# Attention scores as quarter matmuls, gate logits summed once per route group, and moved gate and route products

## The chip, the core and the metric

One core of one Trainium2 chip runs the whole program. The metric is device time in microseconds (us) of one execution. The core has five engines with instruction streams of their own: TensorE (PE, whose weight loads the profile shows as PEld), VectorE (DVE), ScalarE (ACT), GpSimd (POOL) and SyncE (SP, which here only issues transfers). Each runs its own instructions in the order in which they stand, and waits for the others by semaphores. 16 DMA engines move the data.

## The reference

Attention over mean-pooled keys and values, then a mixture of experts with one expert per token. Inputs are f32; tokens are B * S = 4608, in 36 tiles of 128.

```python
batch, n_heads, seq, head_dim = (8, 8, 576, 64)
N, D, E, F = (4608, 512, 8, 1024)

k_p = k.reshape(B, H, Sp, pool, D).mean(axis=3)      # Sp = 72 pooled positions
v_p = v.reshape(B, H, Sp, pool, D).mean(axis=3)
scores = scale * np.matmul(q, k_p.transpose(0, 1, 3, 2))
attn = np.exp(scores - np.max(scores, axis=-1, keepdims=True))
attn = attn / (np.sum(attn, axis=-1, keepdims=True) + 1e-09)
x = np.matmul(attn, v_p)                             # to [4608, 512]

do_compute = (x @ w_skip) > 0
logits = x[do_compute] @ w_gate
e_idx = np.argmax(logits, axis=1)
gate_w = softmax(logits)[chosen]
out = x;  out[do_compute] += gate_w * (relu(xc @ w1[e]) @ w2[e])   # e = e_idx per token
```

## The kernel before

**Attention** runs tile by tile, t = 0 to 35, one loop iteration per tile (line 842). Work of three tiles overlaps in an iteration. PE computes the scores of tile t (L303), the values of tile t - 2 (L341, L344) and the transposes of the probabilities of tile t - 1 (L323, L324). DVE divides tile t - 3 by its sums and takes the row minima (L309) of tile t. ACT copies the transposed probabilities out of PSUM (`turned_p`, L328) and computes the eight exponentials of tile t (L315). Keys stand block-diagonally (`kbd`), two heads per matmul: K = 128 rows of which each head uses 64, 144 columns. A batch is 4.5 tiles, so tiles 4, 13, 22 and 31 hold half of one batch and half of the next; there scores and values are computed for 64 tokens at a time (`parts`), with 64 of the array's columns. An f32 matmul is one instruction in the program and two passes in the profile.

**Per batch** the keys are summed over the pool by DVE (`sum_k`, L208) and the values by POOL (`sums`, L248, then `values_both`, L271), from loads that SP issues seven to eight tiles before the batch's first tile. The value sums are transposed by PE (`turn_v`), copied by ACT (`turned_v`, L267) and multiplied with the gate weights (`gates_pe`, L278; `gates_dve`, L281 and L284), so that the values matmul also gives, per head, the nine gate logits of a token.

**Routing** goes by groups of tiles, `GROUPS = [9, 5, 4, 6, 5, 4, 3]`. `normalised` scales the logits of each tile (L359), writes x to the output and sums the logits over heads into `lg` (L362). When a group's last tile is done, `route` is queued: DVE finds each token's expert, PE counts tokens by matmuls (L397 to L401, the *products*), DVE makes the table positions (`r_di`, L406) and the payment (L408), and POOL writes one table row per token with an indirect DMA per tile (L415), 36 in all. The steps are generators, and `routes.step`, `routes.exponentials` and `routes.products` advance them at fixed places of the iteration.

**What sets the order.** Nothing is reordered on the chip; a small planner in the program decides in which iteration optional work stands. `act`, `dve` and `gps` hold items with a first tile, a last tile and an assumed cost, and each iteration takes items up to a budget (ACT 1.0, DVE 1.5, later 1.0, POOL 3.2). `Spaced.take` for POOL puts table writes between other items, with clears of the ring (L768) as filling late on. All loads are on SP's queue, by `loads[t]` at the start of iteration t.

**After the loop** the last tiles are finished, PE starts on 384 near tokens (`tile_steps`: x against the first expert, three f32r matmuls per step), and `slots` computes from the counts which table rows are needed. POOL gathers them (L1040) when all table writes have landed; PE transposes them (L1072), at a fixed place, behind 84 of the near tokens' matmuls; DVE makes the slot numbers. With these the experts' loop starts, which gathers tokens, multiplies (L1383 to L1409) and scatters results until the end.

## Time and profile before

| | |
|---|---|
| time, median of 3 runs (lowest to highest) | 480.29 us (479.85 to 484.28) |
| the profiled execution: time, span of its instructions | 481.24 us, 479.2 us |
| PE busy, share of the span | 463.5 us, 97% |
| PEld, DVE, ACT, POOL busy | 417.1, 303.4, 225.7, 250.3 us |
| mean granted clock of TensorE | 0.999 of 2.4 GHz |
| DMA moved | 103.88 MB, mean 217 GB/s |

Attention fills the first 147 us; the near tokens and the routing's end reach to about 185 us; the rest is the experts' loop. A row of the timeline gives start, duration, engine, line, operation and tiles, shapes and the number of merged instructions; in brackets stands how long the engine was idle before and for whom it waited. PE's durations include the time until a result is out, so matmuls that follow each other overlap in them; the step from one start to the next is what PE spends on one. Sums of busy time are averages over stages with different limits.

### The profile page before, as it was taken

Reading aid. Unit: us, or ns where it says so; the run is one execution under the profiler, and the core shown is the slowest. Engines: PE = TensorE matmul, PEld = TensorE weight load, DVE = VectorE, ACT = ScalarE, POOL = GpSimd, SP = SyncE. Lnnn points to the kernel's source line nnn. Section 1 sums busy time; section 2 is a strip of 40 time slices with the busy share of each in tenths; the row PEclk is TensorE's granted clock in tenths of the full one; section 3 lists DMA queues with packets and bytes.
Section 4 is the critical chain, followed back from the end, with each engine's and each line's share of the span. In section 5 each row is a group of like instructions: output and inputs, shape, how many; then the busy total and the mean of one; then the engine's idle time right before and its main releaser. Section 6 shows DMA issues by size and latency. Waiting matters only on the chain. (4 is left out here: it accounts for less than half of the span.)

```text
span 479.2 us, 11182 instructions
## 1 busy us (share of the span) xinstructions
PE 463.5 (97%) x3043; PEld 417.1 (87%) x3044; DVE 303.4 (63%) x713; ACT 225.7 (47%) x578; POOL 250.3 (52%) x328
## 2 busy tenths in 40 slices
PE   7999999999999999899999999999999999999995
PEld 4799899989999979798989987989899898989894
DVE  5877888798788622578795667663846554343321
ACT  5678768888891211546462645612435251212110
POOL 4499499999998154363342424362624161515242
PEclk9999999999999999999999999999999999999999
DMA  8999999996931026679787497877687223322021
GB/s 278 388 396 390 361 352 332 384 333 207 328 122 68 11 62 215 230 228 308 247 289 244 136 290 241 300 240 251 202 256 262 89 95 101 129 66 88 22 88 42
DMA packets 52042, 103.88 MB, mean 217 GB/s; under 512 B 10031, under 2 KB 22959, under 8 KB 50336
## 3 DMA queue, kind: packets, MB, share of 16 engines
q1 hardware_dynamic: 40544, 78.18, 47.8%
q0 software_dynamic: 11456, 25.22, 15.0%
q8 instruction: 17, 0.28, 0.2%
q14 instruction: 25, 0.20, 0.1%
HBM read 80.85 MB, written 31.21 MB: 234 GB/s over the span
## 5 line engine op out<-in xcount | busy, mean ns | idle before, releaser
L1289 POOL DMA_INDIRECT out<-ring,slot x33 | 35.8, 1085 | 109.3 <-POOLq L1115 105.6
L315 ACT ACTIVATE e<-sc,mn 128x72 f32<-128x72 f32 x288 | 65.0, 345 | 7.4 <-DVE mn L309 6.8
L1527 ACT ACTIVATE hhi<-psl 128x256 fp32r<-128x256 f32 (+3 forms) x59 | 23.5, 400 | 94.0 <-ACTq L1115 93.5
L1384 PE MATMUL psl<-xlo,w1hi 128*128 128x256 f32 (+3 forms) x220 | 64.1, 291 | 0.0
L1383 PE MATMUL psl<-xhi,w1hi 128*128 128x256 f32 (+3 forms) x220 | 64.0, 291 | 0.0
L1385 PE MATMUL psl<-xhi,w1lo 128*128 128x256 f32 (+3 forms) x220 | 64.0, 291 | 0.0
L1284 POOL DMA_INDIRECT ring<-out,slot x42 | 46.6, 1109 | 22.6 <-issue 22.4
L341 PE MATMUL o<-vbd,pT 128*128 128x148 f32 (+1 forms) x312 | 49.4, 298 | 1.1 <-DVE x L360 1.1
L1626 DVE SCALAR_TENSOR_TENSOR hlo<-psl,hhi 128x256 fp32r<-128x256 f32 (+2 forms) x55 | 23.2, 423 | 41.3 <-DVEq L1115 39.0
L415 POOL DMA_INDIRECT table<-pay,r_di x36 | 36.7, 1018 | 12.6 <-DVE mb L443 6.4
L1383 PEld LDWEIGHTS psl<-xhi,w1hi 128*128 128x128 f32 x220 | 41.3, 188 | 0.8 <-issue 0.4
L1384 PEld LDWEIGHTS psl<-xlo,w1hi 128*128 128x128 f32 x220 | 41.3, 188 | 0.5
L341 PEld LDWEIGHTS o<-vbd,pT 128*128 128x128 f32 (+1 forms) x312 | 38.6, 179 | 3.6 <-ACT ring L213 1.0
L1385 PEld LDWEIGHTS psl<-xhi,w1lo 128*128 128x128 f32 x220 | 41.2, 187 | 0.0
L1297 POOL DMA_DIRECT2D sorted<-ring x39 | 22.2, 572 | 32.9 <-DMA ring<-out,slot 25.8
L1603 DVE TENSOR_TENSOR w2lo<-stage,w2hi 128x1024 fp32r<-128x1024 f32 x28 | 34.3, 1223 | 6.6 <-DVEq L1115 6.4
L1384 PE MATMUL psd<-xlo,w1hi 128*128 128x256 f32 (+3 forms) x132 | 38.4, 291 | 0.0
L1385 PE MATMUL psd<-xhi,w1lo 128*128 128x256 f32 (+3 forms) x132 | 38.4, 291 | 0.0
L1383 PE MATMUL psd<-xhi,w1hi 128*128 128x256 f32 (+3 forms) x132 | 38.4, 291 | 0.0
L1409 PE MATMUL mb<-w2hi,hlo 128*128 128x512 f32 x88 | 34.8, 396 | 0.0
L1409 PE MATMUL psf<-w2hi,hlo 128*128 128x512 f32 x88 | 34.8, 396 | 0.0
L1407 PE MATMUL psf<-w2hi,hhi 128*128 128x512 f32 x88 | 34.8, 395 | 0.0
(276 smaller groups left out, 1216.0 us busy)
## 6 DMA issues: line engine op xcount, KB each, us to landing
stage<-in_w SPq DMA_DIRECT2D x64, 512.0 KB, 5.5
sorted<-ring POOLq DMA_DIRECT2D x39, 256.0 KB, 3.3
out<-x SPq DMA_DIRECT2D x36, 256.0 KB, 5.4
stage<-in_k SPq DMA_DIRECT2D x6, 1152.0 KB, 8.8
blocks<-sorted SPq DMA_DIRECT2D x100, 64.0 KB
qt<-in_q SPq DMA_DIRECT2D x9, 512.0 KB, 7.4
hhi<-in_vm SPq DMA_DIRECT2D x4, 1024.0 KB, 7.7
hlo<-in_vm SPq DMA_DIRECT2D x3, 1024.0 KB, 9.8
```

The source lines that it names most:

```text
L315: nc.scalar.activation(ev[:, h // 2, k0:k0 + SP], sc[:, h * SP:(h + 1) * SP], AF.Exp, bias=mn[:, 4 * i + h:4 * i + h + 1], scale=-1.0)
L341: nc.tensor.matmul(o_[sl, g * 2 * VA:(g + 1) * 2 * VA], pT[:, 2 * a + g, sl], vbd[b % 2][:, 2 * a + g, :], start=(g == 0), stop=False)
L415: m = nc.gpsimd.indirect_dma_start(table, bass.IndirectOffsetOnAxis(ap=di[:, j:j + 1], axis=0), flat(fin["pays"][:, t0 + j:t0 + j + TW // ...
L1284: g.indirect_dma_start(ring[:, (s + 3) % 9, 0:D], None, out, bass.IndirectOffsetOnAxis(ap=slot[:, s:s + 1], axis=0), bounds_check=NTOK - 1 ...
L1289: g.indirect_dma_start(out, bass.IndirectOffsetOnAxis(ap=offsets, axis=0), ring[:, (s + 3) % 9, 0:D], None, bounds_check=NTOK - 1, oob_is_ ...
L1383: t.matmul(ps, whi[0][:, k, w], xhi[:, k, xs], start=(k == 0), stop=False)
L1384: t.matmul(ps, whi[0][:, k, w], xlo[:, k, xs], start=False, stop=False)
L1385: last = t.matmul(ps, wlo[0][:, k, w], xhi[:, k, xs], start=False, stop=(k == 3))
L1407: t.matmul(ps, hhi[:, k, sl], whi[1][:, k, :], start=(k == 0), stop=False)
L1409: last = t.matmul(ps, hlo[:, k, sl], whi[1][:, k, :], start=False, stop=(k == 7))
L1527: a.activation(hhi[:, f, xs], bank(f, xs, alone), AF.Relu).then_inc(sem["act"], 1)
L1603: v.tensor_tensor(chunk_of(wlo, c), chunk_view(stage[c], c), chunk_of(whi, c).bitcast(F32), ALU.subtract).then_inc(sem["wlo1" if c < 4 els ...
```

## The change

Scores of tiles 3 to 33 are computed in quarters. `scores` now issues 16 matmuls per tile in place of 4: for each of four head pairs, two halves of the tokens by two heads, each with 64 rows (one head's dimensions), 64 tokens and 72 columns. The two row halves write two PSUM tiles. The first three and last two tiles keep the old form (`by_halves`). `exped` follows the new places of the heads.

The transposed probabilities are copied in two pieces, of 384 and 256 columns (`turned_p`), into two tiles; the order of the transposes is changed so that the first three fill the first piece. The gate product's PSUM place moves from `mb` to `pt`, and one temporary of the routing from PSUM to SBUF.

`normalised` keeps the scaled logits of a whole group in one tile and sums them over heads once, with the group's last tile.

In the iteration, `routes.exponentials` comes first; `gates_pe` stands behind the values; `gates_dve` moves into the next iteration; the route's products stay before the exponentials only if they were already due at the start of the iteration, and otherwise stand behind the values. The load of the first weight chunk stands behind the tile's output, ACT takes up to two items in the iteration before a batch starts, and assertions state that a chunk's place is free in program order. `slots` cuts its small tiles out of a query buffer.

```diff
+        group = sp.tile([128, GMAX, H, 9], F32, name="l8")
...
+        def by_halves(t):
+            return t < 3 or t > NT - TILES
...
+        def scores(t):
+            if by_halves(t):
+                return [scores_by_halves(t, i) for i in range(2)]
+            sc = [ps_s.tile([128, 512], F32, name="sc")[:, 0:4 * SP] for _ in range(2)]
+            for g in range(4):
+                for i, sl in enumerate(halves):
+                    b = (t * 128 + i * 64) // S
+                    for r, o in zip(halves, range(2)):
+                        nc.tensor.matmul(sc[o][sl, g * SP:(g + 1) * SP], qts[t // QG][r, t % QG, g, sl],
+                                         kbd[b % 2][r, g, o * SP:(o + 1) * SP], start=True, stop=True)
+            return sc
...
         def turn_p(e):
             for i in range(2):
                 k0 = (4 * SP + GAP + 2 * KL) * i
                 ev = e[:, k0:k0 + 256].rearrange("p (k g) -> p g k", g=2)
                 for g in range(2):
-                    nc.tensor.transpose(ptf[:, (2 * i + g) * 128:(2 * i + g) * 128 + 128], ev[:, g], ident)
-            nc.tensor.transpose(ptf[:, 512:640], e[:, 256:384], ident)
+                    nc.tensor.transpose(pt[:, i, (2 * i + g) * 128:(2 * i + g) * 128 + 128], ev[:, g], ident)
+                if i == 0:
+                    nc.tensor.transpose(pt[:, 0, 256:384], e[:, 256:384], ident)

         def turned_p():
-            pT = ap.tile([128, 5, 128], F32, name="pT")
-            nc.scalar.activation(flat(pT), ptf[:, 0:640], AF.Copy)
+            pT = [ap.tile([128, 3 - i, 128], F32, name=f"pT{i}") for i in range(2)]
+            for i, sl in enumerate((slice(0, 384), slice(256, 512))):
+                nc.scalar.activation(flat(pT[i]), pt[:, i, sl], AF.Copy)
             return pT
...
-            nc.vector.tensor_reduce(lg[:, t, :], l8.rearrange("p h c -> p c h"), axis=AX.X, op=ALU.add)
+            if t + 1 in ends:
+                nc.vector.tensor_reduce(lg[:, t0:t + 1], group[:, 0:n8].rearrange("p j h c -> p j c h"), axis=AX.X, op=ALU.add)
...
-            at(wload(cc), lambda cc=cc: load_first(cc))
+            (loads if cc else behind).setdefault(wload(cc), []).append(lambda cc=cc: load_first(cc))
...
             new = turns.get(t)
+            known = routes.held
+            routes.exponentials()
             if t > 3:
                 pts[t - 2] = turned_p()
...
-            routes.exponentials()
             if t > 2:
                 normal(t - 3)
-                sc = [scores(t, i) for i in range(2)]
+                if t - 1 in turns:
+                    gates_dve(turns[t - 1])
+                for f in behind.pop(t, ()):
+                    f()
+                sc = scores(t)
...
-            if new is not None:
-                gates_pe(new)
...
+            elif known:
+                routes.products()
             else:
-                routes.products()
-            spent = act.take(t, 0.4 if new is not None else 0.0, 1)
+                routes.exponentials()
+            spent = act.take(t, 0.4 if new is not None else 0.0, 2 if t + 1 in FIRST[2:] else 1)
             exponentials(t, sc, mn)
             os_[t - 2] = values(t - 2, pts.pop(t - 2))
+            if new is not None:
+                gates_pe(new)
+            fresh = t < NT - 1 and routes.products()
             if 2 < t < NT - 1:
                 turn_p(es.pop(t - 1))
...
             while t < NT - 1 and busy < (DVE if t < PICKED else DVEL) and routes.step():
-                busy += 0.24
+                busy += 9 if fresh else 0.24
```

Two places show what moves. The first is PE's stream at tile 5, where batch 1's gate product is made. `pt` holds transposed probabilities, `sc` scores, `o` values; `vs` and `ls` are value sums, `wgs` the gate weights. Before:

```order
L323 MATMUL pt<-cfs,e_127 128x128 x4
L324 MATMUL pt<-cfs,e_127 128x128
L261 MATMUL pt<-cfs,vs 128x128 x2
L262 MATMUL pt<-cfs,ls_133 128x128
L303 MATMUL sc<-ring,xhi 128x144 x4
L278 MATMUL mb<-wgs,vT 128x36 x3
L341 MATMUL o<-vbd_120,pT 128x148 x2
L344 MATMUL o<-ring,pT 128x2x74
L341 MATMUL o<-vbd_120,pT 128x148 x2
L344 MATMUL o<-ring,pT 128x2x74
```

The same place of the change:

```order
L340 MATMUL pt<-cfs,e_128 128x128 x2
L342 MATMUL pt<-cfs,e_128 128x128
L340 MATMUL pt<-cfs,e_128 128x128 x2
L262 MATMUL pt<-cfs,vs 128x128 x2
L263 MATMUL pt<-cfs,ls_134 128x128
L318 MATMUL sc<-ring,xhi 64x72 x16
L360 MATMUL o<-vbd_120,pT_442 128x148 x2
L363 MATMUL o<-ring,pT_442 128x2x74
L360 MATMUL o<-vbd_120,pT_443 128x148 x2
L363 MATMUL o<-ring,pT_442 128x2x74
L279 MATMUL pt<-wgs,vT 128x36 x3
```

The scores are 16 quarters instead of 4 matmuls, the third transpose is the fifth of before, and the gate product has gone from between scores and values to behind the values.

The second place is POOL's stream around the first table write. `hlo` holds batch 4's loaded values here, `vl` the rest of them; `vbd_121` is the end of batch 3's work. Before:

```order
L271 TENSOR_TENSOR vbd_121<-vs,cfs 128x8x64
L415 DMA table<-pay,r_di 36864x8
L248 TENSOR_TENSOR hlo<-hlo 128x512
L415 DMA table<-pay,r_di 36864x8
L248 TENSOR_TENSOR hlo<-hlo 128x512
L415 DMA table<-pay,r_di 36864x8
```

The same place of the change:

```order
L272 TENSOR_TENSOR vbd_121<-vs,cfs 128x8x64
L249 TENSOR_TENSOR hlo<-hlo 128x512 x2
L249 TENSOR_TENSOR vl_129<-vl_129 96x256
L436 DMA table<-pay,r_di 36864x8
L249 TENSOR_TENSOR hlo<-hlo 128x512
L436 DMA table<-pay,r_di 36864x8
```

Three sums of batch 4 that stood between and behind the first writes now stand ahead of the first one. From there to the gather both streams hold the same number of each kind of instruction.

## Rows read from the trace of the kernel before

**Rows 1.** Windows by stretch: length, busy time of each engine (instructions), clock, DMA, GB/s

```profile
20.00:57.00 37.00, 35.99 (x305) 33.73 (x305) 29.79 (x91) 28.12 (x102) 27.98 (x39) 1.00 1.02 395
180.00:479.00 299.00, 291.71 (x1749) 261.50 (x1748) 166.94 (x263) 108.62 (x183) 115.85 (x151) 1.00 0.56 187
```

**Rows 2.** Around L1072: PE's timeline, the last write, the gather, and their landing times

```profile
146.97 0.43 PE L532 MATMUL sc<-xhi,w1hi 128*128 128x384 f32 x1
155.03 0.98 POOL L415 DMA_INDIRECT table<-pay,r_di  x1 [0.30 <-issue]
table<-pay,r_di POOLq DMA_INDIRECT x1, 2.1
158.10 1.08 POOL L1040 DMA_INDIRECT stage<-table,s_coli  x1 [2.08 <-DVE s_last L1060]
DMA to landing us min/median/max: 4.0/4.0/4.0
162.82 0.34 PE L1072 MATMUL o<-cfs,stage 81*128 81x81 f32 x2
```

**Rows 3.** POOL's stretch of table writes: the window, and its first write

```profile
55.78:156.05 100.27, 98.01 (x820) 92.55 (x819) 83.38 (x302) 75.25 (x251) 92.21 (x108) 1.00 0.76 266
55.78 1.08 POOL L415 DMA_INDIRECT table<-pay,r_di  x1 [6.39 <-DVE mb L443]
```

**Rows 4.** Batch 4's values: issue on SP, landing, first sum on POOL; DMA behind it

```profile
46.89 0.38 SPq L221 DMA_DIRECT2D hlo<-in_vm  x1
hlo<-in_vm SPq DMA_DIRECT2D x1, 1024.0 KB, 9.8
56.90 1.29 POOL L248 TENSOR_TENSOR hlo<-hlo 128x512 f32<-128x512 f32 x1
56.00:58.00 2.00, 2.00 (x25) 1.70 (x24) 1.90 (x9) 1.08 (x3) 1.97 (x2) 1.00 0.68 256
```

**Rows 5.** Timeline of PE and ACT over one undisturbed tile

```profile
67.63 0.27 PE L324 MATMUL pt<-cfs,e 128*128 128x128 f32 x1
67.74 1.15 PE L303 MATMUL sc<-ring,qt 128*128 128x144 f32 x8
68.00 0.70 ACT L328 ACTIVATE pT<-pt 128x640 f32<-128x640 f32 x1 [0.59 <-PE pt L324]
68.76 0.77 PE L341 MATMUL o<-vbd,pT 128*128 128x148 f32 x4
70.37 0.63 PE L323 MATMUL pt<-cfs,e 128*128 128x128 f32 x4
70.84 0.27 PE L324 MATMUL pt<-cfs,e 128*128 128x128 f32 x1
```

**Rows 6.** PE's timeline in half-batch tiles: scores by half widths, values, and back

```profile
56.73 0.27 PE L262 MATMUL pt<-cfs,ls 128*128 128x128 f32 x1
56.94 1.20 PE L303 MATMUL sc<-ring,xhi 128*64 128x144 f32 x16
66.83 0.29 PE L344 MATMUL o<-ring,pT 128*64 128x148 f32 x1
67.05 0.74 PE L323 MATMUL pt<-cfs,e 128*128 128x128 f32 x4
```

**Rows 7.** A wait (us, times, longest), and the small sums by form

```profile
PEld mb L278 <- ACT vT L267: 1.4, 4, 0.4
L362 DVE TENSOR_REDUCE lg<-l 128x9 f32<-128x72 f32 x32 | 8.7, 273 | 0.0
```

**Rows 8.** PE at the start and the end, and the clock of the last stretch

```profile
1.73 5.47 PE L739 MATMUL o<-ring 128*128 128x512 f32 x6 [1.73 <-POOL ring L717]
10.94 1.02 PE L817 MATMUL o<-ring 128*128 128x512 f32 x2
473.89 0.40 PE L1409 MATMUL psf<-w2hi,hlo 128*128 128x512 f32 x1
478.00:479.20 1.20, 0.00 (x0) 0.00 (x0) 0.00 (x0) 0.00 (x0) 0.00 (x0) 0.54 0.34 128
```

More of the change, by code (lines that the diff above doesn't have):

```diff
@@ L348, in normalised @@
             x = ap.tile([128, H, HD], F32, name="x", bufs=5)
-            l8 = ap.tile([128, H, 9], F32, name="l8")
+            t0, n8 = next(ends[e] for e in sorted(ends) if e > t)
+            l8 = group[:, t - t0]
             rc = ap.tile([128, 2, 4], F32, name="rc")
@@ L408, in route @@
                     lambda: nc.vector.reciprocal(pay[:, t0:t0 + n, 1], se)]
-            for a, b in zip(ranked, paid) if last else zip(paid, ranked):
+            for a, b in zip(ranked, paid) if last else (paid, ranked):
                 a()
@@ L670, in take @@
                         break
-        loads, turns = {}, {}
+        loads, behind, turns = {}, {}, {}
+        lows = []
         act, dve, gps = Work(ACT), Work(DVE), Spaced(GPS)
@@ L812, in exponentials @@
             es[t] = ebuf[t % 2]
-            for i in range(2):
-                exped(es[t], sc[i], mn, i)
+            for n in range(2):
+                exped(es[t], sc[n], mn, n, by_halves(t))
         def constant_product():
@@ L836, in attention @@
         gates_dve(0)
-        sc = [scores(2, i) for i in range(2)]
+        sc = scores(2)
         mn = softmax(2, sc)
@@ L852, in attention @@
                 turned_v(new, tp)
-            routes.exponentials()
             if t > 2:
                 normal(t - 3)
-                sc = [scores(t, i) for i in range(2)]
+                if t - 1 in turns:
+                    gates_dve(turns[t - 1])
+                for f in behind.pop(t, ()):
+                    f()
+                sc = scores(t)
             if t == NT - 1:
@@ L954, in attention @@
         spare = lambda: ps_o.tile([128, 2, 512], F32, name="o")[:, 0].rearrange("p (i n) -> p i n", i=4)
-        for wait in slots(tc, nc, c, offs, table, near, bufs, out, fin, ap, spare):
+        for wait in slots(tc, nc, c, offs, table, near, bufs, out, fin, flat(qp.tile([128, QG, 4, 128], F32, name="qt").rearrange("p a g n -> p (a g) n")), spare):
             if wait:
@@ L977, in slots, with new @@
     rows, slot, gate, nti = (fin[n] for n in ("rows", "slot", "gate", "nti"))
-    new = lambda name, dt=F32: p.tile([128, NE], dt, name="s_" + name)
-    n = new("n"); ni = new("ni", I32); half = new("half", I32); odd = new("odd", I32); units = new("units")
-    three = new("three", I32); wide = new("wide", I32); end = new("end"); zero = new("zero"); le = new("le")
-    le1 = new("le1"); w = new("w"); more = new("more")
-    none = new("none"); kind = new("kind"); own = new("own")
-    cf = p.tile([128, 1], F32, name="s_cf")
-    cd = p.tile([128, 1], F32, name="s_cd")
-    ends = p.tile([128, UNITS, NE], F32, name="s_ends", bufs=1)
-    last = p.tile([128, UNITS, NE], F32, name="s_last", bufs=1)
-    short = new("short")
-    row = p.tile([128, UNITS], F32, name="s_row", bufs=1)
-    edge = p.tile([128, UNITS], F32, name="s_edge", bufs=1)
-    col = p.tile([128, 4], F32, name="s_col")
-    coli = p.tile([128, 1], I32, name="s_coli")
+    at = [0]
+    def new(w=NE, dt=F32):
+        at[0] += -(-w // 8) * 8
+        got = p[:, at[0] - -(-w // 8) * 8:][:, 0:w]
+        return got if dt == F32 else got.bitcast(dt)
+    n, units, end, zero, le, le1, w, more, none, kind, own, short = (new() for _ in range(12))
+    ni, half, odd, three, wide = (new(dt=I32) for _ in range(5))
+    cf, cd, col, coli = new(1), new(1), new(4), new(1, I32)
+    row, edge = new(UNITS), new(UNITS)
+    ends, last = (new(UNITS * NE).rearrange("p (u e) -> p u e", e=NE) for _ in range(2))
     nc.vector.memset(zero, 0.0)
```

40 lines of the change are left out of this document (22 added, 18 removed).

## The prediction

> **What bounds the kernel now.** I read the windows by stretch first. PE is busy in 35.99 of 37 us in the early tiles and in 291.71 of 299 us in the experts behind 180 us [rows 1], so whatever moves the start of the experts moves the end, one for one. The question is what sets that start. PE comes out of attention at 146.97 us [rows 2] and fills the time with 84 matmuls of the near tokens. Then, in its own order, stands the transpose of L1072, which reads the rows that POOL's gather of L1040 fetches from the table. POOL may issue that gather only when the last of 36 table writes has landed. So two paths meet at L1072: PE's (attention, then 84 matmuls) and POOL's (table writes, gather). The reader should compare their arrivals: the last write starts at 155.03 and lands 2.1 later, the gather starts at 158.10 and lands 4.0 later, at 162.1; PE reads at 162.82 [rows 2]. The paths are level to within 0.7 us.
>
> How full is POOL's path? From the first table write to the end of the last it is a stretch of 100.27 us (55.78 to 156.05) with POOL busy in 92.21 [rows 3]; the 8.1 left are spread over 108 instructions, and I saw no wait above 0.31 there. Before it POOL stood idle for 6.39 us, waiting for the first route [rows 3]. The second instruction of the stretch, the first sum over batch 4's values (hlo, 56.90), is near its own limit too: its load was issued at 46.89 and landed 9.8 later, at 56.7 [rows 4]. The 16 DMA engines are full (share 1.02 over 20 to 57 us [rows 1]) and fall to 0.68 only behind 56 [rows 4].
>
> **The change on PE.** An undisturbed tile takes 67.63 to 70.84 = 3.21 us from last transpose to last transpose [rows 5]: 0.11 to the scores, 1.02 until the values, 1.61 for the values, 0.47 for four transposes. The scores are 8 passes (an f32 matmul is two) in 1.15 with a tail of 0.29 (the duration of the single half-width matmul of [rows 6] stands for it), so 0.86 / 7 = 0.123 a pass of 144 columns. Quarters make them 32 passes of 72 columns, 0.061 each by scaling, and if the four quarters run at once, 8 steps. No row shows four; the half-batch tiles show two: 16 half-width passes took 1.20 against 1.15 for 8 full ones, 0.05 more [rows 6]. That gives 7 x 0.061 + 0.05 = 0.48. Changing the array's shape costs: 0.21 from the last full transpose to the first half-width matmul instead of 0.11, and 0.22 from the last half-width matmul (148 columns) to the next full one [rows 6]; with 72 columns I take 0.16. New tile: 0.21 + 0.48 + 0.16 + 1.61 + 0.47 = 2.93, 0.28 less. The copy of the probabilities (0.70, ended at 68.70, 0.06 before the values started) was the values' gate [rows 5]; it is split in two, and the first part can start after three of five transposes, so it ends before 2.93 needs it. 31 tiles change (3 to 33). 27 of them save 0.28 = 7.6. Four half-batch tiles already paid for the shape: 0.21 + 0.91 becomes 0.21 + 0.48, 0.43 each = 1.7. The gate products move behind the values, and the route's products too unless they were already due: that takes away waits like the 1.4 for the values' copy [rows 7], which with its smaller neighbours comes to 3.8; I take 3, bounded by 0 and 3.8. Sum on PE: 12.3. Copies, buffers and POOL's sums, for which the transposes of the values wait, will take some of it back: 5 to 12, and I take 6.5.
>
> **The change on DVE and ACT.** 32 of the 36 small sums over heads took 0.273 each [rows 7]; seven larger ones replace them, at most the same 9.8 us in all. DVE is busy in 29.79 of 37 us [rows 1], so the gain lies beside PE's work and I cost it at nothing. If that cover goes, DVE is earlier, not later. ACT's copies move the same 640 columns; even if each half took the whole copy's 0.70 [rows 5], ACT has 37 - 28.12 = 8.9 us free there [rows 1] over some ten tiles, 0.89 each. I cost it at nothing too.
>
> **The change on POOL.** The number of sums, clears and writes from there to the gather is the same. But three sums over batch 4 (two of 512 columns and one of 256) now stand ahead of the first write. Before, POOL could write while that load was on its way. Now it waits for the load, and all of the 100.27 us lies behind it. If the load lands at 56.7 as before, POOL ends at 56.9 + 100.27 = 157.2 instead of 156.05: +1.1. How much earlier can it land? It is issued at the start of tile 11, which PE reaches at most 3.0 earlier (7 x 0.28, one half-batch tile 0.43, two gate waits of 0.3). So the bounds are 53.9 and 56.9. The load has the bytes of all earlier loads ahead of it, and with the engines full an earlier issue only lengthens the queue; so I take 56.6, by the row with share 1.02 [rows 1]. The Trainium skill (DMA: Bandwidth & Descriptors, Queues, rings and completion order) says that the descriptors of one ring are consumed in order; by it alone the load would land at 56.7, and POOL's shift would be +1.1 instead of +0.8. This case's trace agrees as far as the share goes. POOL's shift: +0.8 (bounds -1.9 and +1.1). PE's slack at L1072 is between 0 and 0.7; I take 0.4. Rows are read 0.4 later than now.
>
> **What late rows do to PE.** PE reaches its transpose at 162.8 - 6.5 = 156.3 and waits there until 163.2: some 7 us with no matmul (5.4 to 12.4 by the gain's bounds). The clock does fall after a pause: the last matmul starts at 473.89, and the mean granted clock of 478 to 479.2 is 0.54 of 2.4 GHz [rows 8], which is mostly the lower level, 1.2 GHz. At the start of the kernel six passes of 512 columns took 5.47, where later two took 1.02 [rows 8], so a pass stood at about 0.85 against 0.43, and the start lost 2.7 us. Price of a fall here: 0 to 2.7. I take 2.2, near the start's row, since these matmuls follow each other without a break and should end the slow stretch a bit sooner.
>
> **Sum.** +0.4 +2.2 = +2.6. The profiled execution took 481.24, of which the span is 479.2 and 2.0 lies around it; it stands 0.95 above the median of 480.29. So the span should become 481.8, and the median 482.9.
>
> **Rivals.**
> - *The same path, and the clock holds*: the wait at L1072 is split among earlier ones or the pause is short enough. 480.3 + 0.4 = 480.7. For it: pauses of 1 to 2 us elsewhere leave the clock at 1.00. 0.2.
> - *Faster: batch 4's load lands as early as it is asked for* (53.9). POOL ends 1.9 earlier, the rows are read 2.3 earlier, 478.0. Against it stands the share of 1.02. 0.1.
> - *Faster: PE's gain passes through*, because POOL's path has room that I don't see. 480.3 - 8 = 472. Against it: the paths arrive within 0.7. It decides wherever POOL's stretch shrinks by more than 1.5. 0.06.
> - *Slower, by the array*: the quarters of the two row halves don't run at once. Place: the scores of 27 tiles. Two at a time: 15 x 0.061 + 0.05 = 0.97, a tile of 3.42, +0.21 x 27, 0.06 more in each half-batch tile, -3 for the waits = +2.9, and PE becomes the later path, without a pause: 483.2, 0.09. One after another: 31 x 0.061 + 0.05 = 1.94, +1.18 x 27, 1.03 more in each of the four, -3 = +33: 513, 0.05. It decides once a tile of scores grows by more than 3.4 / 27 = 0.13 over now.
>
> **How the numbers follow.** My forecast has 0.45, the rivals 0.5, something unseen 0.05. The range of 477.5 to 485.5 takes in the forecast with its whole price of a fall, the held clock, the early load and two at a time; the 513, the 472 and the unseen are left out. About 1% (4.8 us) is what a measurement of this kernel can tell from no change. Faster by that, below 475.5: 0.08 (0.06 and a share of the unseen). Slower, above 485.1: 0.15 (0.05, the high ends of the forecast and of two at a time, and a share of the unseen). Within: 0.77.
>
> **What the profile after would show.** Right: tiles of about 2.93 on PE; POOL idle before the first hlo sum until about 56.6, the first table write near 59.9, the last ending near 156.9; a PE wait of 5 to 12 us before the transpose of the fetched rows, and a granted clock below 1 right behind it. Wrong: tiles of 3.2 or more (the array rivals); hlo starting near 54 (the early load); no wait of PE there (POOL's path was not the limit); a wait but a clock of 1.00 (the held clock).

## The result

The kernel before takes 480.18 us (median of 20 runs, 479.2 to 484.28), the changed kernel 484.24 us (20 runs, 480.35 to 487.37). The ratio is 1.0075, with a 95% interval of 1.0058 to 1.0092: the change makes the kernel slower by 4.1 us, 0.75%. The forecast was 482.9, so the direction and the range held. Much of the way there was not the forecast one.

| | before | change |
|---|---|---|
| time, median | 480.18 us | 484.24 us |
| the profiled execution: time, span | 481.24, 479.2 us | 486.19, 484.0 us |
| PE busy | 463.5 us, 97% | 456.5 us, 94% |
| DVE, ACT, POOL busy | 303.4, 225.7, 250.3 us | 303.5, 226.9, 252.5 us |
| mean granted clock | 0.999 | 0.992 |

The profiled execution of the change stands 1.95 us above its median. Two more executions of it were profiled later (below); they took 481.14 and 479.6 us. Each reading of one profile is a reading of one execution. The two later ones lie low: 479.6 is below all 20 runs of the change and 481.14 below all but one. So no execution near the median was profiled, and in that later session the change may have been faster than here; it was timed there in these two executions only.

The mean granted clock of the change's 20 runs is 0.994, where the kernel before has 0.998 in the sessions of the experiments. Over 480 us that makes an estimated 2 of the 4.1 us.

The windows of the change, the columns as in [rows 1]:

```profile
20.00:57.00 37.00, 33.16 (x535) 30.10 (x527) 27.99 (x76) 28.28 (x110) 27.38 (x38) 1.00 1.02 398
100.00:126.00 26.00, 20.26 (x297) 18.74 (x296) 20.77 (x48) 16.93 (x63) 24.25 (x34) 0.87 0.63 214
```

PE is busy in 33.16 us of the early 37, where it was 35.99 [rows 1]: the quarters did take work off PE, but the stretch is full of waits now. Between 100 and 126 us the granted clock is 0.87; the kernel before had 1.00 there.

PE's timeline of the change, at the two long waits of attention, the first near token and the transpose of the fetched rows:

```profile
103.24 0.73 PE L318 MATMUL sc<-ring,qt 64*64 64x72 f32 x32
106.97 0.92 PE L360 MATMUL o<-vbd,pT 128*128 128x148 f32 x4 [3.00 <-DVE x L380]
...
121.58 1.33 PE L360 MATMUL o<-vbd,pT 128*128 128x148 f32 x4 [2.58 <-DVE mb L426]
...
151.57 0.43 PE L553 MATMUL sc<-xhi,w1hi 128*128 128x384 f32 x1
...
167.68 0.34 PE L1103 MATMUL o<-cfs,stage 81*128 81x81 f32 x2
```

The scores are 32 passes, and the values wait 3.00 and 2.58 us for DVE. The near tokens start at 151.57, 4.6 later than before (146.97 [rows 2]); the transpose of the fetched rows starts at 167.68, 4.86 later than before (162.82 [rows 2]). The span has grown by 4.8, and from that transpose to the end both kernels take the same (316.4 and 316.3 us). So in this pair of profiles the whole loss lies ahead of it, where the prediction looked, but PE has no wait there in this execution. It comes late by itself. (In the twelve other profiles this last stretch takes 313.4 to 317.4 us. Executions differ there by as much as the change costs.)

What PE waits for is seen in DVE's timeline of the change:

```profile
102.85 2.99 DVE L613 TENSOR_TENSOR w1lo<-stage,w1hi 128x512 fp32r<-128x512 f32 x1
...
117.45 2.86 DVE L613 TENSOR_TENSOR w1lo<-stage,w1hi 128x512 fp32r<-128x512 f32 x1
```

L613 computes the low parts of the weights (`low_v`): stage minus w1hi, 128 x 512. It takes 2.99 and 2.86 us here. The same instruction in the kernel before took 1.84 and 1.16 (shown with experiment b), and 0.68 elsewhere in both kernels. Behind it stands the division (x, L380, at 106.14 the first time), for which PE's values wait. The second wait is put down to a step of the routing (L426) that follows the division.

POOL's timeline of the change: the beginning of its stretch, what it did beside the first of these, and the end:

```profile
56.42 2.50 POOL L249 TENSOR_TENSOR hlo<-hlo 128x512 f32<-128x512 f32 x2 [7.67 <-DMA hlo<-in_vm]
...
59.76 1.09 POOL L436 DMA_INDIRECT table<-pay,r_di  x1 [0.16 <-DVE mb L464]
...
102.42 0.99 POOL L436 DMA_INDIRECT table<-pay,r_di  x1 [0.17 <-issue]
103.44 0.63 POOL L255 TENSOR_TENSOR ring<-ls,cfs 96x256 f32<-96x256 f32 x1
104.01 1.27 POOL L608 TENSOR_TENSOR w1lo<-stage,w1hi 128x512 fp32r<-128x512 f32 x1
105.45 1.28 POOL L436 DMA_INDIRECT table<-pay,r_di  x1 [0.17 <-issue]
...
130.49 1.27 POOL L608 TENSOR_TENSOR w2lo<-stage,w2hi 128x512 fp32r<-128x512 f32 x1 [1.37 <-ACT w2hi L604]
...
137.16 1.80 POOL L608 TENSOR_TENSOR w2lo<-stage,w2hi 128x512 fp32r<-128x512 f32 x1 [2.55 <-ACT w2hi L604]
...
159.88 0.98 POOL L436 DMA_INDIRECT table<-pay,r_di  x1 [0.30 <-issue]
```

DVE's subtraction begins at 102.85, 0.43 behind a table write of POOL; two operations that read SBUF follow the write without a gap. It ends at 105.84, 0.56 behind the last of the two (105.28), where POOL has a gap of 0.17 us, and the next write takes 1.28 instead of 0.99. The end of POOL's path: the last write starts at 159.88, 4.85 later than before. 0.64 of it is the later start of the stretch (56.42 against 55.78 [rows 3]), and 3.92 are two waits for ACT's w2hi (1.37 and 2.55). ACT makes w2hi at a place of its own per tile, and the tiles come late. Thus PE's path (+4.6) and POOL's (+4.85) are late together.

**Theory 1**, formed from these rows: an operation of DVE with two operands in SBUF and POOL's work shut each other out. The late DVE stalls PE, PE's clock falls, tiles come later, and ACT's w2hi with them. **Theory 2** is the predicted one: POOL's path is late because it starts behind batch 4's load, and PE waits for it with a falling clock. **Theory 3**: the concentrated sum of logits makes DVE late.

### The profile page after: what moved, and what is told of

It is laid out like the page before. It is cut to its first block, busy times and chain, and to the rows that moved or that the text cites. A ratio compares the mean times of both kernels' runs of the same rounds, so it can differ in the third digit from the quotient of the medians.

```text
span 484.0 us, 12622 instructions
## 1 busy us (share of the span) xinstructions
PE 456.5 (94%) x3755; PEld 408.2 (84%) x3756; DVE 303.5 (63%) x684; ACT 226.9 (47%) x614; POOL 252.5 (52%) x328
## 5 line engine op out<-in xcount | busy, mean ns | idle before, releaser
L360 PE MATMUL o<-vbd,pT 128*128 128x148 f32 (+1 forms) x312 | 51.8, 305 | 13.2 <-DVE x L380 5.0
L360 PEld LDWEIGHTS o<-vbd,pT 128*128 128x128 f32 (+1 forms) x312 | 40.6, 184 | 17.1 <-issue 7.4
L324 DVE TENSOR_REDUCE mn<-sc 128x4 f32<-128x288 f32 x72 | 29.8, 450 | 9.5 <-PE sc L318 7.4
```

The costliest lines, as they stand in the source:

```text
L324: nc.vector.tensor_reduce(mn[:, i * 4:i * 4 + 4], sc.rearrange("p (h k) -> p h k", k=SP), axis=AX.X, op=ALU.min)
L360: nc.tensor.matmul(o_[sl, g * 2 * VA:(g + 1) * 2 * VA], pT[a][:, g, sl], vbd[b % 2][:, 2 * a + g, :], start=(g == 0), stop=False)
```

## The experiments

Times are medians; a ratio is to the kernel before in the same session, where it took 480.39 (a to d), 480.22 (e to h) and 480.6 (i to k).

| run | kernel | us | ratio, 95% interval |
|---|---|---|---|
| a | change, first operand of the two subtractions from PSUM | 480.36 | 0.9973 to 1.0019 |
| b | before, the same | 478.97 | 0.9956 to 0.9995 |
| c | change, scores in halves | 483.7 | 1.0037 to 1.0094 |
| d | change, logits summed per tile | 481.98 | 1.0013 to 1.0074 |
| e | a, with early table writes | 481.42 | 0.9997 to 1.0041 |
| f | change, 3 of 15 clears | 477.26 | 0.9911 to 0.9957 |
| g | f, both subtractions on POOL | 477.93 | 0.9946 to 0.9982 |
| h | change, with early table writes | 480.91 | 1.0009 to 1.0047 |
| i | change again, one execution each | 481.14, 479.6 | |
| j | before, 3 of 15 clears | 479.73 | 0.9967 to 0.9997 |
| k | f, the first subtraction on POOL | 477.65 | 0.9911 to 0.9953 |

**a and b: the operand alone.**

```diff
-            nc.vector.tensor_tensor(piece(wlo, cc, i), stage[:, room(cc), i * 512:i * 512 + 512],
-                                    piece(whi, cc, i).bitcast(F32), ALU.subtract)
+            first = stage[:, room(cc), i * 512:i * 512 + 512] if cc not in (2, 3) else mb[:, 500:501].broadcast_to([128, 512])
+            nc.vector.tensor_tensor(piece(wlo, cc, i), first, piece(whi, cc, i).bitcast(F32), ALU.subtract)
...
+        nc.vector.memset(mb[:, 500:501], 0.0)
```

The new operand is one column of zeros in PSUM, read for all 512. So a, b and e leave out the right values of these w1lo pieces.

> The changed kernel, but DVE's two subtractions for w1lo (L613, 2.99 and 2.86 us in the profile of the change) take their first operand from a constant in PSUM and not from the stage in SBUF, so their w1lo pieces hold other values. Same instruction, same size, same place. Theory 1 (POOL and DVE shut each other out for an operation with two SBUF operands; the late DVE stalls PE, the clock falls, ACT's w2hi comes late for POOL): both take 0.65 to 0.8 us, PE's waits of 3.0 and 2.6 us shrink below 1, the granted clock between 100 and 126 us is 1.00, POOL does not wait for w2hi, the last table write starts at 155 to 157 instead of 159.9, and the time is 479 to 481 (3 to 5 less than the change). Theory 2 (the predicted one: POOL's path is later only because it starts behind batch 4's load): the time stays at 484, within 1.

> The kernel before with the same replacement of the first operand of its two subtractions (L589, 1.84 and 1.16 us), whose w1lo pieces hold other values. Theory 1: both take 0.65 to 0.8, PE's one wait of 0.83 us at 105 us goes, and the time moves by -0.8 to 0, since POOL's table writes set when the rows are fetched. Theory 2 expects no change either, within 0.3. If it gains more than 1, the operand costs by itself and not by its place.

The first subtraction of a and one for w2lo in DVE's timeline, and in PE's the first near token and the transpose of the fetched rows:

```profile
99.96 0.68 DVE L614 TENSOR_TENSOR w1lo<-mb,w1hi 128x512 fp32r<-128x512 f32 x1
...
116.93 3.23 DVE L614 TENSOR_TENSOR w2lo<-stage,w2hi 128x512 fp32r<-128x512 f32 x1
```

```profile
144.03 0.43 PE L553 MATMUL sc<-xhi,w1hi 128*128 128x384 f32 x1
...
163.21 0.42 PE L1104 MATMUL o<-cfs,stage 81*128 81x81 f32 x2 [2.18 <-issue]
```

Both subtractions are short now (0.68 and 0.69 us), at the same place of the program. What POOL did beside them differs from the change: a table write at 99.90, and two sums of 2.51 us together at 110.87. That the operand makes the difference is seen in b. The w2lo parts still read the stage, and one of them takes 3.23 us here, longer than any in the change; PE waits 1.88 us behind it, where theory 1 had expected less than 1. The time falls from 484.24 to 480.36, 3.9 less than the change, as theory 1 expected, and no wait for w2hi is left on POOL. The 3.9 compares two sessions, since the change was not timed beside a. The mean granted clock of a's 12 runs is 0.998; c and d, variants of the change in the same session without this edit, have 0.994 and 0.993. What is left in this profile is theory 2's picture: PE has its near tokens from 144.03 on, comes to the transpose early, and waits 0.47 and 2.18 us for the rows; the clock stays at 1.00 there.

In b the gain is 1.2 us by the ratio (0.2 to 2.1) and 1.4 by the medians, somewhat more than the expected 0 to 0.8. The kernel before pays for the same collision, as its DVE and POOL timelines show:

```profile
102.76 1.84 DVE L589 TENSOR_TENSOR w1lo<-stage,w1hi 128x512 fp32r<-128x512 f32 x1
```

```profile
102.76 1.28 POOL L585 TENSOR_TENSOR w1lo<-stage,w1hi 128x512 fp32r<-128x512 f32 x1
104.21 1.27 POOL L415 DMA_INDIRECT table<-pay,r_di  x1 [0.17 <-issue]
```

The same places of b:

```profile
102.37 0.68 DVE L590 TENSOR_TENSOR w1lo<-mb,w1hi 128x512 fp32r<-128x512 f32 x1
```

```profile
102.37 1.29 POOL L585 TENSOR_TENSOR w1lo<-stage,w1hi 128x512 fp32r<-128x512 f32 x1
103.83 1.01 POOL L415 DMA_INDIRECT table<-pay,r_di  x1 [0.17 <-issue]
```

In both kernels the subtraction begins together with the same operation of POOL's. Before, it runs behind that operation (1.84) and stretches the next write to 1.27; in b it takes 0.68, and the write 1.01. So it is the first operand's place that made it long. (That it is also a single column, read 512 times, was not separated from that.) The expectation put a gain above 1 down to the operand by itself, whatever POOL does. The rows speak against this reading: with both operands in SBUF the subtractions for w2lo take 0.68 before. Against b, then, all the rest of the change costs 480.36 - 478.97 = 1.4 us (two kernels of one session, each with its own interval).

**c: the scores in halves.**

```diff
         def by_halves(t):
-            return t < 3 or t > NT - TILES
+            return True
...
-                nc.tensor.matmul(sc[:, g * 2 * SP:(g + 1) * 2 * SP], qts[t // QG][:, t % QG, half * 2 + g],
-                                 kbd[t * 128 // S % 2][:, half * 2 + g, :], start=True, stop=True)
+                for sl, b in parts(t):
+                    nc.tensor.matmul(sc[sl, g * 2 * SP:(g + 1) * 2 * SP], qts[t // QG][:, t % QG, half * 2 + g, sl],
+                                     kbd[b % 2][:, half * 2 + g, :], start=True, stop=True)
```

> The changed kernel with the scores of all tiles in the old form (4 matmuls of 144 columns per tile, 64 tokens at a time in half-batch tiles). Undisturbed tiles go back to 3.2 us. Theory 1: time follows the collisions; with another phase of DVE against POOL one or both subtractions are shorter than 2.5, and the time is 480 to 483. Theory 2: POOL's start moves by 0.3 at most, so 483 to 485. If the quarters themselves were the loss (weight loads, more instructions), 480.5.

It takes 483.7. Theory 1 expected 480 to 483 with shorter subtractions; they are short (0.68 and 1.09), and yet it is no faster than the change within the intervals, and lies where theory 2 had it (483 to 485). The windows of PE's wait ahead of the fetched rows, and behind it, say why:

```profile
161.93:164.69 2.76, 0.01 (x1) 0.03 (x1) 0.00 (x0) 0.49 (x1) 0.00 (x0) 1.00 0.15 40
164.69:169.50 4.81, 4.81 (x18) 4.65 (x19) 1.57 (x6) 0.49 (x1) 0.00 (x0) 0.65 0.00 0
```

PE does nothing for 2.76 us, and its clock is 0.65 for the 4.81 us behind. From the transpose to the first step behind the slots it is 7.7 us (164.69 to 172.39), where it was 6.38 in the kernel before (162.82 to 169.20) and 6.5 in the change: 1.2 to 1.3 lost to the clock. The last write starts at 157.14, 2.1 later than before. This is the predicted mechanism, in the execution of another kernel. So the loss can be reached in two ways, neither theory alone covers all runs, and quarters are not needed for it.

**d: logits per tile.**

```diff
-            if t + 1 in ends:
-                nc.vector.tensor_reduce(lg[:, t0:t + 1], group[:, 0:n8].rearrange("p j h c -> p j c h"), axis=AX.X, op=ALU.add)
+            nc.vector.tensor_reduce(lg[:, t, :], l8.rearrange("p h c -> p c h"), axis=AX.X, op=ALU.add)
```

> The changed kernel with the logits summed over heads per tile again (36 sums of 0.27 us instead of 7 of up to 1.3). Theory 3 (the one long sum at a group's end comes in front of the row minima and makes DVE late just where the routing is due): 481 to 482. Theory 1: this sum stands behind the first collision and is no cause; DVE has 0.27 more in every tile, and the time is 483.5 to 486, unless the collisions move.

481.98 is what theory 3 expected; theory 1 had 483.5 to 486. But its profile does not carry theory 3: the first subtraction is as long as ever (3.05 us) and PE waits 3.05 for it; the second takes 1.29 only, and the clock does not fall. DVE's timeline of d, and its windows at PE's wait and behind it:

```profile
102.15 3.05 DVE L612 TENSOR_TENSOR w1lo<-stage,w1hi 128x512 fp32r<-128x512 f32 x1
```

```profile
103.28:106.33 3.05, 0.00 (x1) 0.03 (x1) 3.02 (x6) 1.14 (x4) 2.85 (x4) 1.00 0.64 249
106.33:110.00 3.67, 3.67 (x55) 3.37 (x56) 3.34 (x13) 2.73 (x11) 3.17 (x8) 1.00 0.74 221
```

The transpose of the fetched rows starts at 162.71 in d, earlier than in a (163.21). So in this execution a collision of 3.05 us and PE's wait behind it, with the clock at 1.00, cost nothing by then. Whether the shorter second collision and the clock are all of the 2.3 us against the change is open; other runs of d lost clock (0.993 in the mean).

**e and h: the first table writes ahead of batch 4's sums**, the order of before, by one condition:

```diff
-                busy += 9 if fresh else 0.24
+                busy += 9 if fresh and t > 14 else 0.24
```

> The changed kernel with DVE's two subtractions for w1lo reading their first operand from PSUM (as in the experiment a_psum_low, and so with other values in those pieces), and one number more: the routing may go on with its steps in the iteration of its products for the first group, so that POOL's first table writes stand ahead of and between the three sums over batch 4 again, in the order of the kernel before. Theory 2 (POOL's path through the writes and the gather holds the end once the collisions are gone, and it is late because it starts behind batch 4's load at 57.0 us): the first write starts near 55, the last 1.0 to 1.7 earlier than the 155.69 of a_psum_low, PE's waits ahead of the transpose of the fetched rows (0.47 and 2.18 us there) shrink to 1 to 1.6 together, and the time is 478.8 to 479.6. If the start of POOL's path is no limit, it stays at 480.4.

e took 481.42, not 478.8 to 479.6. In its profile the whole program is 2 us late from early on (a wait of PE for DVE that ends at 20.95 in a ends at 22.97): the granted clock is 0.50 from 11 to 13 us, where a has 1.00. By the near tokens 0.3 of it is left (144.34 against 144.03). The last write starts at 155.88, which counted from that early wait is 1.8 earlier than in a, as expected; but PE's wait stays (0.35 and 2.40) and the clock falls behind it, to 0.64 from 163.62 to 168.40. To the first step behind the slots it is 8.05 us from the transpose, in a 6.56. Its runs lie in two groups, 478.7 to 479.7 (four of 12) and 480.9 to 483.5. Whether POOL's start limits the end could not be settled with it.

> The kernel of g_low_on_pool with the first table writes ahead of batch 4's sums, as in e_psum_low_early_writes. Theory 1 and 2 together: 0.5 to 1.5 faster than g_low_on_pool, 477.5 to 479.5, and faster than the kernel before by 0.2 to 0.6%. If POOL's start is no limit: the same as g_low_on_pool.

By a mistake the kernel that ran under h is not the one that this text describes: the two subtractions stayed on DVE and all 15 clears stayed, so h is the change with early writes alone, and the numbers of the text don't apply. It took 480.91, 3.3 less than the change. The subtractions take 0.68 and 1.08 in its profile, and PE waits 3.02 us for the fetched rows without a fall of the clock. So this one profile, too, has no long collision of the two. The first table write starts at 56.00 and the last at 155.32, 0.8 to 1.1 ahead of the executions of i (below) and 0.3 later than before: with the order of before, POOL's path is nearly back, as theory 2 has it.

The mistake makes e and h a pair of one session that differ in the operand alone: 481.42 with it in PSUM, 480.91 with it in SBUF. Here the operand gains nothing. So a and h stand 3.9 and 3.3 below the change's 484.24 by different edits, and both edits together (e) no lower. Neither is shown to take away the one cause. Had the change itself taken 480 to 481 in these sessions, as its two executions under i did, the picture would be the same.

**f and g: room on POOL.**

```diff
-                        if self.apart < REST and self.fill:
+                        if self.apart < REST and self.fill and len(cleared) < 3:
```

and for g also

```diff
-            if cc > 1 and i:
+            if cc > 3 and i:
                 dve.add(now["t"] + 1, now["t"] + 2, 0.65, lambda: low_v(cc, i))
                 return
             gps.add(now["t"] + (2 if cc > 4 else 1), (NT if cc > 5 else wload(cc + 3)) - 1, 1.25, lambda: low(cc, i))
```

> The changed kernel with 3 of POOL's 15 filling clears (0.55 us each, a write with a clear takes 1.69 us, one without 1.29). POOL's stretch shrinks by up to 12 x 0.40 = 4.8 us. Theory 1: PE too comes late to the transpose of the fetched rows, through its two waits, at 167.7, and the waits for w2hi and the routing of the last group stay: the time moves by less than 1 (483.3 to 484.5). If POOL's path alone holds the end, 479.5 to 481.

> The changed kernel with DVE's two subtractions for w1lo given to POOL (1.28 us each there), and 3 filling clears instead of 15, which makes room for them (12 x 0.40 = 4.8 us). Theory 1: nothing of DVE collides with POOL in the tiles, PE's waits of 3.0 and 2.6 us shrink below 1, the clock stays at 1.00 between 100 and 126 us, the last write starts at 153 to 156, and the time is 478 to 480.5. If the collisions were only where a general lateness of DVE showed, PE's waits stay above 2 and the time above 482.

g took 477.93, just under the expected 478 to 480.5. It holds f's edit and is no faster than f, so moving the subtractions gained nothing more there. f refutes what theory 1 said of it: 477.26 in place of 483.3 to 484.5; it is below the other case (479.5 to 481) too. The clears that it leaves out repeat: all 15 go over the same three places. In its profile, DVE's and POOL's timelines at the first subtraction, and PE's and POOL's at the fetched rows:

```profile
102.50 0.68 DVE L613 TENSOR_TENSOR w1lo<-stage,w1hi 128x512 fp32r<-128x512 f32 x1
```

```profile
102.57 1.49 POOL L436 DMA_INDIRECT table<-pay,r_di  x1 [0.17 <-DMA xlo<-in_q]
...
154.80 1.07 POOL L1071 DMA_INDIRECT stage<-table,qt  x1 [2.08 <-DVE qt L1083]
```

```profile
144.46 0.43 PE L553 MATMUL sc<-xhi,w1hi 128*128 128x384 f32 x1
...
160.55 0.34 PE L1103 MATMUL o<-cfs,stage 81*128 81x81 f32 x2
```

Up to here the program is that of the change. But the subtraction starts 0.07 us ahead of the table write instead of 0.43 behind it; it takes 0.68, and it is the write that is stretched (1.49 against 0.99). The near tokens start at 144.46, the gather at 154.80, and the fetched rows are there when PE comes at 160.55, without a wait. So PE's gain of 2.3 us passes through once POOL's path is shorter than PE's.

**i: the change twice more.** f suggested that the collision is not the program's but the execution's.

> The changed kernel itself, unchanged, for one more profile. Theory 1 in its sharper form: whether DVE's subtraction at 102.5 us starts just ahead of POOL's table write (then it takes 0.7 us and the write up to 1.5, as in f_three_clears) or a few tenths into it (then it waits for the write and the two operations behind it and takes about 3 us) is a matter of 0.1 to 0.5 us, which differs between executions of one program. So its duration here is either under 1.2 or over 2.5, and the profiled execution takes 480.5 to 483 in the first case and 483.5 to 487 in the second. If the collision belongs to the program, it takes 2.99 again.

> The same once more, with the same two cases: under 1.2 us and 480.5 to 483, or over 2.5 us and 483.5 to 487.

The first subtraction in DVE's timeline, of the first execution, then of the second:

```profile
100.36 1.43 DVE L613 TENSOR_TENSOR w1lo<-stage,w1hi 128x512 fp32r<-128x512 f32 x1
```

```profile
104.25 1.96 DVE L613 TENSOR_TENSOR w1lo<-stage,w1hi 128x512 fp32r<-128x512 f32 x1
```

One program, and the first subtraction takes 2.99, 1.43 and 1.96 us; in the first of these two a third one (w2lo) takes 2.80. That there are only two cases, under 1.2 and over 2.5, was wrong, and so was the second time (479.6, below either case); that it differs between executions is shown. Both are faster than the kernel's median. POOL's last table write in the first of them, and the windows at PE's wait for the fetched rows and behind it:

```profile
156.38 1.17 POOL L436 DMA_INDIRECT table<-pay,r_di  x1 [0.30 <-issue]
```

```profile
161.17:163.90 2.73, 0.00 (x1) 0.04 (x1) 0.00 (x0) 0.49 (x1) 0.00 (x0) 1.00 0.16 41
163.90:166.00 2.10, 2.10 (x13) 2.10 (x14) 1.39 (x5) 0.00 (x0) 0.00 (x0) 1.00 0.00 0
```

PE waits 2.73 us (and 0.45 shortly before), the clock stays at 1.00 behind it, and the transpose starts at 163.90. In the second execution the clock falls twice, to 0.50 from 11 to 13 us and to 0.57 from 98.02 to 102.00, behind a wait of 2.05 for DVE. Its near tokens start at 147.26, 3.05 later than in the first, and yet it is the faster of the two: POOL's path is as late in both (the transpose starts at 164.00), and from there to the end it takes 313.4 us against 315.2. Why that stretch is shorter is open.

**j and k.** j is the kernel before with f's edit; k is f with `cc > 1 and i and cc != 2`, so that POOL computes the first subtraction only.

> The kernel before with 3 of its 15 filling clears on POOL, so that POOL's table writes end up to 4.8 us earlier. The prediction read that PE and POOL meet at the transpose of the fetched rows within 0.7 us. If so, PE's order holds it and the time falls by 0 to 0.7, 479.5 to 480.4. If POOL alone held the end of the kernel before, 476 to 478.

> The changed kernel with 3 of 15 filling clears, as f_three_clears, and with the first of DVE's two subtractions for w1lo given to POOL (1.28 us there). It computes all of the reference's work. Theory 1: no collision at 102 us in any execution, attention ends at 142.5 to 144.5, the gather starts near 155.5, and the time is 476.5 to 477.8 with a spread under 3, against 477.26 and a spread of 3.7 in f_three_clears. If the time is above 478, POOL's path is the later one again.

The gather of j in POOL's timeline, and the transpose of the fetched rows in PE's:

```profile
157.30 1.08 POOL L1040 DMA_INDIRECT stage<-table,s_coli  x1 [2.08 <-DVE s_odd L1052]
```

```profile
162.86 0.34 PE L1072 MATMUL o<-cfs,stage 81*128 81x81 f32 x2
```

In j the gather starts 0.8 earlier than before (158.10 [rows 2]), PE comes to the transpose at 162.86, when it did before, and the time falls by 0.03 to 0.33%, as expected: PE's order holds that place, and the paths of the kernel before are level, as read. The edit did not take the up to 4.8 us off POOL's end, since the writes of the last groups then wait for the routing (3.60 and 1.11 us); so j tries the 0.8 only. k took 477.65, as expected and as fast as f, but its runs spread over 5.3 us (474.7 to 480.03), not under 3, and in its profile the near tokens start at 145.88, not by 144.5.

f and k are faster than the kernel before by 0.4 to 0.9%; f is the change with 12 memsets fewer.

## Why the forecast came out

**Level paths at the transpose of the fetched rows:** right. j shortened POOL's path alone, by 0.8, and gained next to nothing; in the first profile of the change the whole loss shows as a later transpose.

**The array:** right. Four quarters run at once: 32 passes start within 0.51 us (0.48 forecast): the 0.73 of the row at 103.24 less the 0.22 of the last pass. An undisturbed tile takes 2.99 us (2.93 forecast) from one third transpose to the next in the change's PE timeline:

```profile
34.97 0.27 PE L342 MATMUL pt<-cfs,e 128*128 128x128 f32 x1
...
37.96 0.27 PE L342 MATMUL pt<-cfs,e 128*128 128x128 f32 x1
```

**PE's gain, 5 to 12 us and 6.5 taken:** wrong. The window from 20 to 147 us of the kernel before, then of the first execution of i, whose near tokens start at 144.21:

```profile
20.00:147.00 127.00, 124.28 (x1061) 117.04 (x1059) 104.77 (x337) 101.40 (x348) 111.40 (x136) 1.00 0.87 317
```

```profile
20.00:147.00 127.00, 116.72 (x1784) 107.19 (x1773) 106.13 (x319) 102.71 (x382) 110.32 (x135) 1.00 0.88 321
```

Before, PE is busy in 124.28 of these 127 us; in this execution in 116.72, and attention ends 2.76 earlier. So 7.56 + 2.76 = 10.3 us of work went, near the 9.3 forecast (12.3 less 3 for waits), but only 2.8 were kept; in the second execution of i 0.3 were lost (147.26), with two falls of the clock in it, and in the first profile 4.6. The step that failed is the one that put DVE's part at nothing because DVE is busy in 29.79 of 37 us: a share over a stretch, where the tile decides. DVE's timeline of an ordinary tile of the change:

```profile
39.25 0.82 DVE L324 TENSOR_REDUCE mn<-sc 128x4 f32<-128x288 f32 x2 [0.24 <-PE sc L318]
...
40.94 0.21 DVE L375 RECIPROCAL rc<-o 128x8 f32<-128x8 f32 x1 [0.21 <-PE o L363]
...
41.33 0.68 DVE L380 TENSOR_TENSOR x<-o,rc 128x512 f32<-128x512 f32 x1
42.58 0.82 DVE L324 TENSOR_REDUCE mn<-sc 128x4 f32<-128x288 f32 x2 [0.57 <-PE sc L318]
```

From one pair of row minima to the next it is 3.33 us here; DVE waits 0.21 and 0.57 of them for PE, and some 2.55 are work (0.74 of it a key sum, L209) in an order from which PE needs the last (x) for its next values. With a tile of 2.99 some 0.4 us are free. Steps of the routing or a subtraction of 0.68 stand out by what exceeds that, and PE waits, as here in the change's PE timeline:

```profile
53.70 0.74 PE L360 MATMUL o<-vbd,pT 128*128 128x148 f32 x4 [1.25 <-DVE r_oh L411]
...
65.53 0.72 PE L360 MATMUL o<-vbd,pT 128*64 128x148 f32 x8 [1.32 <-DVE njt L486]
```

The kernel before has one wait above 0.5 for DVE in all of attention (0.83). DVE's idle time was real, but in this tile it is waiting for PE (0.21 and 0.57), and only the 0.4 is room.

**POOL's shift, +0.8 within -1.9 to +1.1:** right in kind, in size at its upper bound or a little above. The first sum of batch 4 starts at 56.42, 56.61 and 56.60 in the three profiles (56.6 taken), the first table write at 59.76, 59.96 and 59.95 (59.9), and the last starts at 156.38 and 156.12 where POOL did not wait for w2hi, 1.1 to 1.35 later than before. The load was issued at 45.79 and 45.25 in the first two of these profiles, 1.1 and 1.6 earlier than before, and the sum that waits for it starts only 0.3 and 0.1 ahead of the landing before (56.7): the earlier issue gained little, as forecast. The prediction's +1.1 for a landing at 56.7 is a slip, since the sum can start with the landing; it makes +0.9. A start that the bytes ahead of the load set and one that the ring's order sets differ by 0.1 here (56.6 and 56.7), which these rows cannot tell apart.

**PE's wait and the clock, 5.4 to 12.4 us and +2.2:** wrong in size. Since PE kept 2.8 at most, it waits 3.2 us (0.45 + 2.73) and 0.5 in the two executions of i and not at all in the first profile, and the clock falls in none of the three at this place. It falls so in c, for 1.2 to 1.3, and in e, for 1.5. The prediction's price came from the start of the kernel (5.47 for six passes), but the profile gives a granted clock of 1.00 from 1.70 to 7.30 us there, so that row is not shown to be a fall. In the change's first profile it falls inside attention, behind the two waits for DVE. The windows behind the waits, each with the same work of another tile beside it:

```profile
106.97:111.19 4.22, 4.22 (x20) 4.04 (x20) 3.56 (x11) 1.81 (x8) 3.65 (x10) 0.60 0.60 200
126.00:128.58 2.58, 2.58 (x21) 2.41 (x21) 2.18 (x6) 2.54 (x11) 2.31 (x4) 1.00 0.99 264
121.58:125.25 3.67, 3.67 (x18) 3.55 (x18) 2.11 (x8) 1.81 (x8) 3.33 (x5) 0.61 0.73 225
100.96:103.24 2.28, 2.28 (x18) 2.16 (x18) 1.79 (x4) 2.03 (x9) 2.12 (x4) 1.00 1.02 362
```

4.22 against 2.58 and 3.67 against 2.28 us: two falls of the clock cost 1.6 and 1.4.

**What the sum lacked:** the collisions of DVE's subtractions with POOL, which the trace of before held (1.84 and 1.16 for an instruction that takes 0.68 elsewhere) and the forecast neither read nor priced. a, without the two for w1lo, is 3.9 us below the change, across sessions; b is 1.4 below the kernel before, in one session. The rest of the change costs 1.4 (a against b), where the forecast had +0.4 to +2.6. The clock did cost the change an estimated 2 us over its 20 runs, near the +2.2, but where its profiles show it fall, it falls inside attention (and at the start), not at the transpose. So a sum of +2.6 came near a measured +4.1 with its largest term, the clock, in the wrong place, and without the collisions: the direction and the range held by luck as far as the mechanism goes. The rival "the clock holds" (480.7) is what a and the first execution of i show in time and clock.

What stays open:

- Whether the change takes 484 in other sessions at all, and with it how much of the differences to a, f and h is their edit. f stands 7.0 us below the change, where its shorter POOL path shows 3.3 (163.90 to 160.55, f against the first of i) and its one profile has no long collision at the two places; a change of 480 to 481 in f's session would leave just that.
- Which of the late tiles, POOL's later start and the clock makes up the 4.1 in an execution near the median. The collisions are shown as a cost in b and as the delay of one execution of the change, not as the cause of the median.
- How often an execution of the change meets which collision (three profiles, three cases).
- Why the clock falls at the start of some executions (e and the second of i).

## What to carry to other kernels

An engine's spare time has to be read in the cycle it works in, between the result it waits for and the one that is waited for, and not as a share of a stretch: a shorter step on the bound engine uses up exactly that spare time. Where an instruction has several durations for one shape in a profile (0.68, 1.16 and 1.84 here), look for who shuts it out before moving anything, since a shift of some tenths can turn the small loss into the large one, and differently in each execution. When two paths are level, take work off both; f took 12 fillers off POOL, and the gain on PE came through. And time the unchanged kernel again beside its variants: differences of 3 to 7 us are read across sessions here, and two later executions of the same kernel were 3 to 5 us faster than its median.

## What the runs showed of the hardware

- **DVE and POOL shut each other out for a DVE operation with two SBUF operands.** 128 x 512 took 0.68 us undisturbed and up to 3.23 us beside POOL (a); begun together with the same operation of POOL's it took 1.84 before and 0.68 in b, with the first operand from PSUM. The Trainium skill (SBUF — State Buffer, Who interferes with whom) says that such an instruction contends with a GpSimd instruction that reads SBUF, and that issue order decides which of the two waits. The trace agrees with that, and shows two things more: DVE waited not for one instruction but for up to three of POOL in a row (2.99 us), until a gap of 0.17 us came; and an indirect table write, too, is held up by DVE: in f one that started 0.07 us behind such a subtraction took 1.49, in e one that started 0.08 us behind a subtraction from PSUM took 0.99.
- **Four quarters of the array work at once**: 32 passes of 72 columns on 64 rows and 64 columns of the array started within 0.51 us.
- **After a pause of PE the clock fell or held at like lengths.** Its mean was 0.57 to 0.65 of 2.4 GHz, so mostly the lower level, in the stretches behind pauses of 3.00 and 2.58 (change), 2.76 (c), 2.40 (e) and 2.05 us (the second of i), and it stayed at 1.00 behind 3.05 (d), 3.02 (h), 2.73 (the first of i) and 2.01 us (f). A forecast can give such a fall a chance and a price (1.2 to 1.6 us here), not a certainty.
